# Four buffers for the transposed squares, four slots for the mirrored blocks, and side work moved in the first chunk and the last batch of an attention-and-experts kernel

## The chip, the core and the metric

The kernel runs on one core of a Trainium2 chip. The core has a matrix engine (TensorE, PE in the profile; PEld is its weight load), a vector engine (DVE), an activation engine (ACT), a general engine (POOL) and a sync engine (SP) that issues nearly all DMAs here, in one queue and in program order. The metric is the device time of one execution in microseconds. Before the change the median of three runs is 1546.55 us (1545.86 to 1554.03).

## What is computed

```python
# _attn_ref: batch 8, seq 2496, d_model 256, d_qk 64, all float32
scores = (1 / S) * np.matmul(z, z.transpose(0, 2, 1))
attn = np.maximum(scores, 0.0) ** 2
x = u * np.matmul(attn, v)                     # 19968 rows of 256
# _moe_ref: 8 experts, F = 1024, capacity 80
logits = x @ w_gate;  expert_idx = np.argmax(logits, axis=1)
# gate_w: the softmax probability of the chosen expert
for e in range(E):
    tok_idx = np.where(expert_idx == e)[0]     # cut to the 80 rows with ties broken as argpartition does
    h = np.maximum(x[tok_idx] @ w1[e], 0.0)
    out[tok_idx] = gate_w[tok_idx, None] * (h @ w2[e])
```

The matrix of scores is symmetric in z, and nothing but relu, square and a scale follows, so a block of squares below the diagonal is the transpose of one above it.

## The kernel before

The 2496 rows of a batch are padded to 20 tiles of 128. A **chunk** is four tiles (512 query columns), so a batch has five chunks; the names (b, qc) give batch and chunk, and there are 40. A chunk is worked off in ten **steps** r, each for a **pair** of key tiles (k = 2r, 2r+1). In the text "the second chunk" is qc = 1, and so on.

`scores(b, qc, k)` makes one pair. If the pair lies on or above the diagonal, PE multiplies (lines 300 and 301: two matmuls per tile, because z is split into a rounded part and a rest; `zc` holds the two in its halves, `zd` the same crossed), ACT does relu and square (304, 305), and the square `a` is split into `ah` (a rounding copy, on ACT or DVE) and `al` (a subtraction on DVE, line 310). Above the diagonal `mirror` also transposes the square on DVE (line 248) into a tile `x`, which four tiles of keys fill; the full `x` of 1 MB goes to DRAM as `y` (line 253), and is read back as a block `blk` (line 266) for the chunk in which it stands below the diagonal. There `mirrored` takes the place of the scores: ACT copies `blk` to `ah` (284), DVE subtracts to `al` (286). A block is named by (b, i, j): written in chunk j, used in chunk i. So chunk 0 writes (1,0), (2,0), (3,0), (4,0); chunk 1 writes (2,1), (3,1), (4,1); chunk 2 (3,2), (4,2); chunk 3 (4,3). `attend` multiplies `v` (split into two parts in `vt`) by `ah` and `al`: twelve matmuls for a pair and chunk (331 to 333).

Scores run two steps ahead (`LOOK = 2`). At each step the loop emits, in this order: the reads of blocks that are due, the scores of step i + 2, the attends of step i, the work on the chunk that just ended (`finished`: x = u * out, its rounding for the logits, a DMA transpose to 16-bit rows and their store, the logits, the gate), loads and splits for later chunks, the zeroing of a piece of the output, and in the last two chunks the early loads and splits of expert weights (`weights_ahead`, table `WAT`). The order on PE, ACT, DVE and SP is the order of this code (`manual_schedule`); each engine works off its own list and waits where a buffer or an input isn't ready.

The tiles that the change touches: `x` has two buffers (`sqpool`), a block takes one of six slots (`free`, `slot_of`), `y` has four buffers in DRAM, and a read of a block is emitted two steps after its write was. `prep_zd` fills `zd` of the next chunk with two DMAs from `zc` (lines 119, 120) at step 4. `prep_zc` (111) and `prep_v` (144, 145) split z and v. When the last chunk ends, `chunk_x_last`, `chunk_logits_last` and the last gate follow, and then the stage of the experts.

Of the kernel before, what the change touches and what calls it, by code (L numbers as in the profile page):

```python
# [8 lines left out]
F32 = mybir.dt.float32  # L9
# [10 lines left out]
P = 128  # L20
# [5 lines left out]
def attn_moe_kernel(ctx, tc, zT, uT, v, wg, w1, w2, out, seq, cap):  # L26
# [5 lines left out]
    nc = tc.nc  # L32
# [32 lines left out]
    NV, NW, NR = 6, 2, 5  # L65
    NA = 6
    SQ = 32
    weights = ExitStack()
    vpool = weights.enter_context(tc.tile_pool(name="vpool", bufs=NV))
    apool = weights.enter_context(tc.tile_pool(name="apool", bufs=1))  # L70
    sqpool = weights.enter_context(tc.tile_pool(name="sqpool", bufs=2))
    main = ExitStack()
# [100 lines left out]
    raw12 = upool.tile([P, 2, CH], F32, tag="ut", name="raw12")  # L173
    nc.sync.dma_start(out=raw12, in_=zT[0, :, CH:3 * CH].rearrange("p (j t) -> p j t", j=2))
    vraw0 = load_v(0, 0)


# [55 lines left out]


    a_t = {}

    half_t, blk, slot_of, free = {}, {}, {}, list(range(NA))
    n32 = P // SQ  # L240
    moving, now = [], [0]

    def mirror(b, i, j, t, a):

        if t == 0:
            half_t[b, i, j] = sqpool.tile([P, n32, QT, QT, SQ], F32, tag="x", name=f"x_{b}_{i}_{j}")
        x = half_t[b, i, j]
        V.transpose(out=x[:, :, :, t].rearrange("p n k s -> p k n s"), in_=a)  # L248
        if t < QT - 1:
            return  # L250

        y = dram.tile([n32, SQ, n32, QT * QT * SQ], F32, tag="y", name=f"y_{b}_{i}_{j}", bufs=4)
# [36 lines left out]
    def scores(b, qc, k):  # L289
# [262 lines left out]
    def wtile(name):  # L552
        if late.get("own"):
            pool, tag = late["own"], "w"
        else:
            i = n_early[0] % (NA + 2 + NV + NW)
# [39 lines left out]
    NP = NT // 2  # L596
    LOOK = 2
# [11 lines left out]
    def weights_ahead(b, qc, r):  # L609
        for p, raw in list(w_raw.items()):  # L610
            split_w(*p, w_raw.pop(p), V)
        if (b, qc, r) in WAT:
            if not places:

                assert len(free) == 3
                order = [free.pop() for _ in range(2)] + [slot_of[b, NQ - 1, j] for j in range(3)]
                places.extend([(apool, f"a{n}") for n in order[:2]] + [(sqpool, "x")] * 2)
                places.extend([(apool, f"a{n}") for n in order[2:4]] + [(vpool, "vt")] * 2)
                places.extend([(apool, f"a{n}") for n in order[4:] + free] + [(vpool, "vt")] * (NV - 2))
            p = WAT[b, qc, r]  # L620
            w_raw[p] = load_raw(*p)

    def finished(b, qc, r):

        if r == 0:
            chunk_hi(b, qc)
        elif r == 1:
            chunk_rest(b, qc)
            chunk_store(b, qc)
        elif r == 2:  # L630
            chunk_mid(b, qc)
        elif r == 3:
            chunk_lo(b, qc)
            chunk_store2(b, qc)
        elif r == 6:
            chunk_logits(b, qc)
            chunk_sum(b, qc)
# [6 lines left out]
        elif qc == 0 and b > 0:  # L644
            part = kb - BPB, kb
            if r == 2:
                count(*part)
            elif r == 4:
                up_to(*part)
                blocks(ps_m, "m", gp, oh, *part)  # L650
        elif b == B - 1 and qc == NQ - 2:
            part = kb, kb + BPB - 2
            if r == 7:
                gate_top(b, 0, NQ - 1)
                gate(b, 0, NQ - 1)
            elif r == 8:
                count(*part)
                up_to(*part)
                half()
            elif r == 9:  # L660
                blocks(ps_m, "m", gp, oh, *part)

    with tc.manual_schedule(engines={ET.PE, ET.Activation, ET.DVE, ET.SP}):
# [6 lines left out]
        z_raw[0, 2] = raw12[:, 1]  # L670
        z_raw[0, 3] = load_z(0, 3)
        v_raw[0, 1] = load_v(0, 1)
        constants()
        prev = None
        for i, (b, qc, r) in enumerate(steps):
            last = b == B - 1 and qc == NQ - 1
            now[0] = i
            mirror_back(i)
            if r == 0 and prev:
                chunk_x(*prev)  # L680
            if i + LOOK < len(steps):
                nb, nqc, nr = steps[i + LOOK]
                scores(nb, nqc, 2 * nr)
            if b == 0 and qc == 0:
                if r % 2 == 0 and r < 8:
                    g = r // 2 + 1
                    prep_v(0, g, v_raw.pop((0, g)), V, V)
                    if g + 1 < NQ:
                        v_raw[0, g + 1] = load_v(0, g + 1)
                if r % 2 == 1 and r < 6:  # L690
                    j = r // 2 + 2
                    prep_zc(0, j, z_raw.pop((0, j)))
                    if 3 < j + 1 < NQ:
                        z_raw[0, j + 1] = load_z(0, j + 1)
                if r == 8:
# [30 lines left out]
            if r == NP - 1:  # L726
                prev = b, qc
# [558 lines left out]
```

## Time and profile before

| | |
|---|---|
| median of three runs | 1546.55 us |
| the profiled execution | 1546.61 us |
| its span on the core | 1544.9 us |
| first chunk | 0 to 70.6 us |
| the other 38 chunks of the loop's steady part | 70.6 to 1401.7 us |
| last chunk | 1401.7 to 1444.8 us |
| end of the last chunk to the end of the span | 100.1 us |

The end of a chunk is the end of its last attend on PE (line 336). The profiled execution's time is 1.7 us more than its span, which is the work around it. All times in the rows below count from the span's start.

### The profile page before, as it was taken

How to read it: one execution, taken by the hardware profiler on the slowest of the kernel's cores; microseconds unless marked ns; L12 is line 12 of the kernel's file. 1: busy time of each engine (PE TensorE's matmuls, PEld its weight loads, DVE VectorE, ACT ScalarE, POOL GpSimd, SP SyncE). 2: the span in 40 equal slices, each digit the busy share in tenths (PEclk: the TensorE clock that was granted, in tenths of full speed). 3: DMA queues.
4: the chain of work that ended last, by engine and by line, in shares of the span. 5: the costliest groups of instructions: out<-in, count | busy, mean ns of one | idle time of the engine just before them, and what ended most of it. 6: DMA issues, size and time to landing. Idle time of an engine off the chain costs nothing. (4 is left out here: it accounts for less than half of the span.)

```text
span 1544.9 us, 19497 instructions
## 1 busy us (share of the span) xinstructions
PE 1416.7 (92%) x7083; PEld 1160.8 (75%) x7083; DVE 1085.0 (70%) x1538; ACT 979.9 (63%) x1254; POOL 48.5 (3%) x51
## 2 busy tenths in 40 slices
PE   6899999899989999899989999899989999898577
PEld 4688887788768877688768877788868887786356
DVE  5776777677866778567866767667767768666575
ACT  4476677557656677566666676566776667565254
POOL 1000000000000000000000000000000000000064
PEclk8899999999999999999999999999999999999699
DMA  4779859986898959887799959999599859988454
GB/s 143 211 212 246 197 146 186 250 226 161 247 196 233 234 135 193 234 241 189 199 190 249 218 135 219 230 237 225 155 210 245 226 132 232 218 218 254 83 182 142
DMA packets 300102, 311.97 MB, mean 202 GB/s; under 512 B 136184, under 2 KB 228224, under 8 KB 289760
## 3 DMA queue, kind: packets, MB, share of 16 engines
q1 hardware_dynamic: 299040, 309.11, 80.3%
q0 software_dynamic: 960, 1.56, 0.3%
q8 instruction: 57, 0.93, 0.3%
q14 instruction: 45, 0.37, 0.1%
HBM read 153.48 MB, written 126.46 MB: 181 GB/s over the span
## 5 line engine op out<-in xcount | busy, mean ns | idle before, releaser
L333 PE MATMUL acc<-al,vt 128*128 128x512 f32 (+1 forms) x1520 | 596.1, 392 | 48.0 <-DVE al L54 47.8
L331 PE MATMUL acc<-ah,vt 128*128 128x512 f32 (+1 forms) x1520 | 595.2, 392 | 1.4 <-ACT ah L284 0.8
L332 PE MATMUL acc<-ah,vt 128*128 128x512 f32 (+1 forms) x1520 | 593.1, 390 | 0.0
L54 DVE TENSOR_TENSOR al<-a,ah 128x1024 fp32r<-128x1024 f32 (+1 forms) x240 | 290.9, 1212 | 137.2 <-ACT ah L104 127.7
L333 PEld LDWEIGHTS acc<-al,vt 128*128 128x128 f32 x1520 | 291.1, 192 | 112.3 <-DVE al L54 58.8
L304 ACT ACTIVATE a<-s 128x512 f32<-128x512 f32 (+1 forms) x480 | 259.1, 590 | 147.3 <-PE s L301 135.6
L331 PEld LDWEIGHTS acc<-ah,vt 128*128 128x128 f32 x1520 | 291.7, 192 | 60.5 <-ACT ah L284 5.8
L332 PEld LDWEIGHTS acc<-ah,vt 128*128 128x128 f32 x1520 | 291.2, 192 | 54.9
L284 ACT CAST ah<-blk 128x1024 fp32r<-128x1024 f32 x160 | 166.1, 1047 | 180.9 <-DMA blk<-y 99.6
L248 DVE STREAM_TRANSPOSE x<-a 128x512 f32<-128x512 f32 x320 | 207.7, 687 | 76.2 <-DMA y<-x 76.2
L305 ACT ACTIVATE a<-a 128x1024 f32<-128x1024 f32 (+1 forms) x240 | 252.9, 1054 | 7.6
L54 DVE TENSOR_TENSOR al<-blk,ah 128x1024 fp32r<-128x1024 f32 x160 | 191.5, 1213 | 66.1 <-ACT ah L284 62.5
L301 PE MATMUL s<-zd,zc 128*128 128x512 f32 (+1 forms) x480 | 190.7, 397 | 16.3 <-DMA zd<-zc 16.3
L300 PE MATMUL s<-zc,zc 128*128 128x512 f32 x320 | 131.6, 411 | 21.0 <-DVE zc L54 19.5
L104 ACT CAST ah<-a 128x1024 fp32r<-128x1024 f32 x136 | 142.8, 1050 | 4.3
L106 DVE CAST ah<-a 128x1024 fp32r<-128x1024 f32 (+1 forms) x104 | 70.8, 681 | 92.1 <-ACT a L305 91.8
L301 PEld LDWEIGHTS s<-zd,zc 128*128 128x128 f32 x480 | 92.1, 192 | 35.3 <-DMA zd<-zc 19.0
L300 PEld LDWEIGHTS s<-zc,zc 128*128 128x128 f32 x320 | 60.8, 190 | 35.8 <-issue 21.1
L361 ACT CAST xb<-xf 128x1024 bf16<-128x1024 f32 (+1 forms) x39 | 40.0, 1027 | 58.6 <-DVE xf L350 58.6
L300 PE MATMUL s<-zc 128*128 128x512 f32 (+1 forms) x160 | 64.3, 402 | 1.7 <-ACT a L304 1.7
L145 DVE TENSOR_TENSOR vt<-vraw,vt 128x1024 fp32r<-128x1024 f32 (+1 forms) x39 | 45.6, 1168 | 25.6 <-ACT vt L104 25.2
L104 ACT CAST vt<-vraw 128x1024 fp32r<-128x1024 f32 (+3 forms) x50 | 40.4, 835 | 33.8 <-DMA vraw<-v 33.8
(158 smaller groups left out, 867.3 us busy)
## 6 DMA issues: line engine op xcount, KB each, us to landing
y<-x SPq DMA_DIRECT2D x80, 1024.0 KB, 7.4
blk<-y SPq DMA_DIRECT2D x320, 256.0 KB, 5.8
out<-idle SPq DMA_DIRECT2D x40, 512.0 KB, 6.6
vraw<-v SPq DMA_DIRECT2D x32, 512.0 KB, 6.2
ut<-uT SPq DMA_DIRECT2D x32, 512.0 KB, 4.6
xs<-xq SPq DMA_DIRECT2D x32, 512.0 KB, 6.5
wraw<-w SPq DMA_DIRECT2D x32, 512.0 KB, 5.5
zd<-zc SPq DMA_DIRECT2D x78, 128.0 KB, 7.1
```

Of the source, the lines that this page charges most:

```text
L54: V.tensor_tensor(out=o, in0=a, in1=b, op=op)
L104: eng.copy(out=o, in_=i)
L106: eng.tensor_copy(out=o, in_=i)
L248: V.transpose(out=x[:, :, :, t].rearrange("p n k s -> p k n s"), in_=a)
L284: nc.scalar.copy(out=natural(ah), in_=src)
L300: nc.tensor.matmul(s[:, :nq], zk, zc[:, :nq], start=True, stop=False)
L301: nc.tensor.matmul(s[:, :nq], zk, zd[:, :nq], start=False, stop=True)
L304: nc.scalar.activation(out=a[:, h, :nq], in_=s[:, :nq], func=AF.Relu)
L305: nc.scalar.activation(out=a[:, :, :nq], in_=a[:, :, :nq], func=AF.Square)
L331: nc.tensor.matmul(o, vt[:, t, 0, cs], ah, start=k == 0, stop=False)
L332: nc.tensor.matmul(o, vt[:, t, 1, cs], ah, start=False, stop=False)
L333: nc.tensor.matmul(o, vt[:, t, 0, cs], al, start=False, stop=False)
```

## The change

The buffers: `x` gets four instead of two, the slots of blocks become four instead of six, `y` in DRAM gets twelve. A read of a block is no longer emitted by age alone: reads go in the order of use, when the write is two steps old, when a slot is free, and at most twelve steps before the block is used; and `mirror_back` stands at the end of a step instead of its start. The list `to_read` runs, within a batch, in the order (1,0), (2,0), (2,1), (3,0), (3,1), and so on; its last number is the step in which the block's first pair is split.

```diff
-    NA = 6
+    NA = 4
+    NX = 4
-    sqpool = weights.enter_context(tc.tile_pool(name="sqpool", bufs=2))
+    sqpool = weights.enter_context(tc.tile_pool(name="sqpool", bufs=NX))
+    LOOK, AHEAD = 2, 12
+    to_read = [(b, i, j, ((b * NQ + i) * NT + j * QT) // 2 - LOOK)
+               for b in range(B) for i in range(NQ) for j in range(i)]
...
-        moving.append((b, i, j, y, now[0] + 2))
-
-    def mirror_back(i_step):
-
-        while moving and moving[0][4] <= i_step:
-            b, i, j, y, _ = moving.pop(0)
+        y_t[b, i, j] = y, now[0]
+
+    def mirror_back():
+
+        while to_read and free:
+            b, i, j, use = to_read[0]
+            if (b, i, j) not in y_t or y_t[b, i, j][1] + 2 > now[0] or use > now[0] + AHEAD:
+                return
+            to_read.pop(0)
+            y = y_t.pop((b, i, j))[0]
             slot_of[b, i, j] = free.pop(0)
...
-            if nb < B and r == 4:
+            if nb < B and r == 1:
                 prep_zd(nb, nqc)
...
+            mirror_back()
             if r == NP - 1:
```

In the first chunk z and v are loaded in other pieces and earlier, `zc` is made two steps before the scores that use it and ahead of them on DVE, the rounding copy of `v` goes from DVE to ACT, the first subtraction of `v` from POOL to DVE, and the three `ah` that DVE made in the first chunk of each batch (`ON_V`) go to ACT in batch 0.

```diff
-        on_v = k // QT == qc or (qc, k) in ON_V
+        on_v = k // QT == qc or (qc, k) in ON_V and b > 0
...
         prep_zd(0, 0, raw0)
+        prep_zc(0, 1, raw12[:, 0])
         scores(0, 0, 0)
+        prep_v(0, 0, vraw0, nc.scalar, V)
         scores(0, 0, 2)
-        prep_v(0, 0, vraw0, nc.scalar, nc.gpsimd)
-        prep_zc(0, 1, raw12[:, 0])
...
+            if (b, qc) == (0, 0) and r in (0, 2, 4):
+                prep_zc(0, r // 2 + 2, z_raw.pop((0, r // 2 + 2)))
             if i + LOOK < len(steps):
...
-                    prep_v(0, g, v_raw.pop((0, g)), V, V)
+                    prep_v(0, g, v_raw.pop((0, g)), nc.scalar, V)
...
-                if r == (7 if b == 0 and qc == 0 else 1):
+                if r == 1:
```

In the last batch the early weights come at other steps (ten pieces: four in the fourth chunk and six in the fifth, where two and eight were), the tiles that they take over are listed anew (`places`), and the work on the fourth chunk, its logits and its gate come one to two steps earlier.

```diff
-    at_w = [(NQ - 2, 6), (NQ - 2, 8)] + [(NQ - 1, r) for r in range(8)]
+    at_w = [(NQ - 2, r) for r in (2, 4, 6, 8)] + [(NQ - 1, r) for r in range(1, 7)]
...
+        at_end = b == B - 1 and qc == NQ - 2
...
-            if r == 7:
+            if r == 5:
                 gate_top(b, 0, NQ - 1)
+            elif r == 6:
                 gate(b, 0, NQ - 1)
```

What this does to the lists of the engines, at three places. The first is SP in the second chunk of batch 1 and the end of its first chunk; `y_2_1` is the write of block (2,1), `blk_2_1` its read, `gall` the gate's values, `xq` the transposed 16-bit rows, `out` the zeroing. Before:

```order
L266 DMA blk_3_0_1968<-y_3_0_1898 32x4x512 x4
L253 DMA y_4_0_1989<-x_4_0_1927 128x2048
L489 DMA xs<-gall 128x20x1 x2
L266 DMA blk_4_0_2043<-y_4_0_1989 32x4x512 x4
L400 DMA_TRANSPOSE xq_0_2126<-xf_0_2065 128x8x128 x2
L99 DMA zraw_2129<-zT 128x512
L158 DMA ut_1_2165<-uT 128x2x512
L253 DMA y_2_1_2183<-x_2_1_2145 128x2048
L409 DMA xs<-xq_0_2126 128x8x256
L543 DMA wtab<-wb_2242 80x256
```

Now, in the same stretch and a little further:

```order
L261 DMA y_4_0_1983<-x_4_0_1921 128x2048
L501 DMA xs<-gall 128x20x1 x2
L412 DMA_TRANSPOSE xq_0_2115<-xf_0_2054 128x8x128 x2
L100 DMA zraw_2118<-zT 128x512
L120 DMA zd_2_2120<-zc_2_1146 64x512
L121 DMA zd_2_2120<-zc_2_1146 64x512
L159 DMA ut_1_2157<-uT 128x2x512
L261 DMA y_2_1_2175<-x_2_1_2137 128x2048
L421 DMA xs<-xq_0_2115 128x8x256
L555 DMA wtab<-wb_2234 80x256
L261 DMA y_3_1_2253<-x_3_1_2205 128x2048
L278 DMA blk_2_1_2268<-y_2_1_2175 32x4x512 x4
```

The reads of (3,0) and (4,0) no longer stand ahead of the write of (2,1), the two DMAs of `zd` do, and the read of (2,1) now stands behind the write of (3,1) (before, it stood ahead of it).

The second is DVE in the first chunk of batch 0, from the first pair's `ah` on. Before:

```order
L106 CAST ah_0_0_149<-a_0_0_139 128x1024
L54 TENSOR_TENSOR al_0_0_151<-a_0_0_139,ah_0_0_149 128x1024
L106 CAST ah_0_2_163<-a_0_2_153 128x1024
L54 TENSOR_TENSOR al_0_2_165<-a_0_2_153,ah_0_2_163 128x1024
L111 CAST zc_1_170<-raw_109 128x512
L54 TENSOR_TENSOR zc_1_170<-raw_109,zc_1_170 64x512
```

Now:

```order
L112 CAST zc_1_144<-raw_109 128x512
L54 TENSOR_TENSOR zc_1_144<-raw_109,zc_1_144 64x512
L107 CAST ah_0_0_157<-a_0_0_147 128x1024
L54 TENSOR_TENSOR al_0_0_159<-a_0_0_147,ah_0_0_157 128x1024
L146 TENSOR_TENSOR vt_0_161<-vraw_0_111,vt_0_161 128x4x256
L107 CAST ah_0_2_174<-a_0_2_164 128x1024
```

`zc_1`, which the third pair's scores need, went from behind two pairs to ahead of the first, and the subtraction of `v` came in from POOL.

The third is SP in the fifth chunk of batch 0, where `zd` of the next batch's first chunk is made. Before:

```order
L99 DMA zraw_1470<-zT 128x512
L131 DMA vraw_2_1475<-v 128x4x256
L158 DMA ut_4_1494<-uT 128x2x448
L409 DMA xs<-xq_3_1467 128x8x256
L131 DMA vraw_3_1517<-v 128x4x256
L119 DMA zd_0_1535<-zc_0_536 64x512
L120 DMA zd_0_1535<-zc_0_536 64x512
```

Now:

```order
L100 DMA zraw_1469<-zT 128x512
L132 DMA vraw_2_1474<-v 128x4x256
L120 DMA zd_0_1476<-zc_0_525 64x512
L121 DMA zd_0_1476<-zc_0_525 64x512
L159 DMA ut_4_1496<-uT 128x2x448
L421 DMA xs<-xq_3_1466 128x8x256
L132 DMA vraw_3_1519<-v 128x4x256
```

`zd` moved ahead of three transfers.

## Rows read from the trace of the kernel before

**Rows 1.** Waits, whole span: us in total, times, longest us.

```profile
DVE x L248 <- DMA y<-x: 76.2, 14, 9.3
PE acc L333 <- DVE al L54: 47.8, 22, 6.4
PE s L300 <- DVE zc L54: 19.5, 4, 8.2
PE s L301 <- DMA zd<-zc: 16.3, 7, 2.9
```

**Rows 2.** Windows, second chunks of batches 1 to 7: us, busy (count), PEclk, DMA.

```profile
410.60:455.90 45.30, 38.05 (x181) 29.77 (x180) 31.61 (x55) 29.13 (x39) 0.00 (x0) 0.93 0.91 205
...
sum 309.20, PE 265.91 PEld 208.09 DVE 220.16 ACT 203.76 POOL 0.00; mean PE 37.99 PEld 29.73 DVE 31.45 ACT 29.11 POOL 0.00
```

**Rows 3.** Windows, second chunk of batch 0.

```profile
70.60:105.40 34.80, 34.80 (x175) 28.70 (x175) 26.93 (x36) 27.29 (x35) 0.00 (x0) 1.00 0.81 212
```

**Rows 4.** Timeline of DVE, second chunk of batch 2: start, us, what [idle before].

```profile
430.05 1.30 DVE L248 STREAM_TRANSPOSE x<-a 128x512 f32<-128x512 f32 x2
...
437.79 1.30 DVE L248 STREAM_TRANSPOSE x<-a 128x512 f32<-128x512 f32 x2
...
449.52 1.30 DVE L248 STREAM_TRANSPOSE x<-a 128x512 f32<-128x512 f32 x2 [9.32 <-DMA y<-x]
```

**Rows 5.** Timeline of SP's DMA queue, the same chunk.

```profile
419.53 7.96 SPq L489 DMA_DIRECT2D xs<-gall  x2
...
431.15 9.57 SPq L400 DMA_TRANSPOSE xq<-xf  x2
...
441.94 0.39 SPq L253 DMA_DIRECT2D y<-x  x1
...
449.51 1.76 SPq L266 DMA_DIRECT2D blk<-y  x4
```

**Rows 6.** Timeline of ACT, start of the third chunk of batch 2.

```profile
459.04 1.05 ACT L284 CAST ah<-blk 128x1024 fp32r<-128x1024 f32 x1 [12.86 <-DMA blk<-y]
```

**Rows 7.** Windows, fifth chunks of batches 0 to 6.

```profile
345.60:375.60 30.00, 28.39 (x159) 25.60 (x159) 21.91 (x24) 20.20 (x25) 0.00 (x0) 1.00 0.90 221
...
sum 223.50, PE 206.81 PEld 185.26 DVE 152.98 ACT 141.15 POOL 0.00; mean PE 29.54 PEld 26.47 DVE 21.85 ACT 20.16 POOL 0.00
```

**Rows 8.** Windows, first chunk of batch 0 from its first attend on.

```profile
17.80:70.60 52.80, 41.48 (x148) 32.70 (x147) 34.78 (x54) 24.16 (x30) 0.00 (x0) 0.82 0.66 183
```

**Rows 9.** Timeline of all engines, first chunk: first relu, first attend.

```profile
6.39 1.09 ACT L304 ACTIVATE a<-s 128x512 f32<-128x512 f32 x2 [2.19 <-PE s L301]
...
17.81 0.63 PE L331 MATMUL acc<-ah,vt 128*128 128x512 f32 x1
```

**Rows 10.** Lines by form: count, busy us, mean ns, idle before.

```profile
L54 DVE TENSOR_TENSOR al<-a,ah 128x1024 fp32r<-128x1024 f32 x224 | 273.4, 1221 | 136.1 <-ACT ah L104 127.7
...
L305 ACT ACTIVATE a<-a 128x1024 f32<-128x1024 f32 x224 | 237.6, 1061 | 7.1
L248 DVE STREAM_TRANSPOSE x<-a 128x512 f32<-128x512 f32 x320 | 207.7, 687 | 76.2 <-DMA y<-x 76.2
...
L104 ACT CAST ah<-a 128x1024 fp32r<-128x1024 f32 x136 | 142.8, 1050 | 4.3
...
L54 DVE TENSOR_TENSOR zc<-zraw,zc 64x512 fp32r<-64x512 f32 x38 | 26.2, 689 | 1.3
...
L111 DVE CAST zc<-zraw 128x512 fp32r<-128x512 f32 x38 | 15.9, 417 | 5.0 <-DMA zraw<-zT 5.0
```

**Rows 11.** Windows, third chunk of batch 2.

```profile
455.90:489.30 33.40, 33.40 (x168) 27.50 (x167) 22.82 (x27) 23.14 (x29) 0.00 (x0) 0.99 0.90 254
```

**Rows 12.** Windows, last chunk.

```profile
1401.70:1444.80 43.10, 31.55 (x156) 25.17 (x156) 31.16 (x48) 21.62 (x26) 0.00 (x0) 0.92 0.69 179
```

**Rows 13.** Timeline of ACT around the end of the last chunk.

```profile
1451.92 1.04 ACT L584 CAST w1h<-wraw 128x1024 fp32r<-128x1024 f32 x1 [12.60 <-DMA wraw<-w]
```

**Rows 14.** Timeline of DVE, the last chunk's x.

```profile
1454.14 1.27 DVE L350 SCALAR_TENSOR_TENSOR xf<-acc,ut 128x256 f32<-128x256 f32 x4
```

More of the change, by code (lines that the diff above doesn't have):

```diff
@@ L173, in attn_moe_kernel @@
     raw12 = upool.tile([P, 2, CH], F32, tag="ut", name="raw12")
-    nc.sync.dma_start(out=raw12, in_=zT[0, :, CH:3 * CH].rearrange("p (j t) -> p j t", j=2))
+    nc.sync.dma_start(out=raw12[:, 0], in_=zT[0, :, CH:2 * CH])
     vraw0 = load_v(0, 0)
+    nc.sync.dma_start(out=raw12[:, 1], in_=zT[0, :, 2 * CH:3 * CH])
+    vraw1 = load_v(0, 1)
+    raw34 = xpool.tile([P, 2, CH], F32, tag="xf", name="raw34")
+    nc.sync.dma_start(out=raw34, in_=zT[0, :, 3 * CH:].rearrange("p (j t) -> p j t", j=2))
     ident = const.tile([P, P], F32, name="ident")
@@ L232, in zero_out @@
                           in_=zero.rearrange("p (o d) -> p o d", o=1).broadcast_to([P, r1 - r0, D]))
+    LOOK, AHEAD = 2, 12
     a_t = {}
-    half_t, blk, slot_of, free = {}, {}, {}, list(range(NA))
+    half_t, y_t, blk, slot_of, free = {}, {}, {}, {}, list(range(NA))
     n32 = P // SQ
-    moving, now = [], [0]
+    now = [0]
+    to_read = [(b, i, j, ((b * NQ + i) * NT + j * QT) // 2 - LOOK)
+               for b in range(B) for i in range(NQ) for j in range(i)]
     def mirror(b, i, j, t, a):
@@ L250, in mirror @@
             return
-        y = dram.tile([n32, SQ, n32, QT * QT * SQ], F32, tag="y", name=f"y_{b}_{i}_{j}", bufs=4)
+        y = dram.tile([n32, SQ, n32, QT * QT * SQ], F32, tag="y", name=f"y_{b}_{i}_{j}", bufs=12)
         nc.sync.dma_start(out=y.rearrange("g p h f -> (g p) (h f)"),
                           in_=x.rearrange("p h k t s -> p (h k t s)"))
-        moving.append((b, i, j, y, now[0] + 2))
-    def mirror_back(i_step):
-        while moving and moving[0][4] <= i_step:
-            b, i, j, y, _ = moving.pop(0)
+        y_t[b, i, j] = y, now[0]
[6 more added lines that the diff above has]
+            y = y_t.pop((b, i, j))[0]
             slot_of[b, i, j] = free.pop(0)
@@ L555, in wtile @@
         else:
-            i = n_early[0] % (NA + 2 + NV + NW)
+            i = n_early[0] % (NA + NX + NV + NW)
             n_early[0] += 1
@@ L596, in attn_moe_kernel @@
     NP = NT // 2
-    LOOK = 2
     ON_V = {(0, 8), (0, 12), (0, 16)}
     order_w = [(0, 1), (0, 2), (1, 1), (1, 2), (2, 1)]
-    at_w = [(NQ - 2, 6), (NQ - 2, 8)] + [(NQ - 1, r) for r in range(8)]
+    at_w = [(NQ - 2, r) for r in (2, 4, 6, 8)] + [(NQ - 1, r) for r in range(1, 7)]
     WAT = {(B - 1,) + at: (*order_w[n // 2], n % 2) for n, at in enumerate(at_w)}
@@ L613, in weights_ahead @@
             if not places:
[L615 to L619, printed above, removed]
+                xt, vv = (sqpool, "x"), (vpool, "vt")
+                nb = B * NQ * (NQ - 1) // 2
+                a4 = [(apool, f"a{n % NA}") for n in range(nb - NA, nb)]
+                places.extend([xt, xt, xt, vv, a4[0], vv, xt, a4[1], a4[2], vv, a4[3], vv, vv, vv])
             p = WAT[b, qc, r]
@@ L629, in finished @@
             chunk_store(b, qc)
-        elif r == 2:
+        elif r == 3:
+            chunk_store2(b, qc)
+        if r == 1 and at_end or r == 2 and not at_end:
             chunk_mid(b, qc)
-        elif r == 3:
+        if r == (2 if at_end else 3):
             chunk_lo(b, qc)
-            chunk_store2(b, qc)
-        elif r == 6:
+        if r == (4 if at_end else 6):
             chunk_logits(b, qc)
@@ L650, in finished @@
                 blocks(ps_m, "m", gp, oh, *part)
-        elif b == B - 1 and qc == NQ - 2:
+        elif at_end:
             part = kb, kb + BPB - 2
-            if r == 7:
+            if r == 5:
                 gate_top(b, 0, NQ - 1)
+            elif r == 6:
                 gate(b, 0, NQ - 1)
@@ L665, in attn_moe_kernel @@
         prep_zd(0, 0, raw0)
+        prep_zc(0, 1, raw12[:, 0])
         scores(0, 0, 0)
+        prep_v(0, 0, vraw0, nc.scalar, V)
         scores(0, 0, 2)
-        prep_v(0, 0, vraw0, nc.scalar, nc.gpsimd)
-        prep_zc(0, 1, raw12[:, 0])
-        z_raw[0, 2] = raw12[:, 1]
-        z_raw[0, 3] = load_z(0, 3)
-        v_raw[0, 1] = load_v(0, 1)
+        v_raw[0, 1] = vraw1
+        z_raw.update({(0, 2): raw12[:, 1], (0, 3): raw34[:, 0], (0, 4): raw34[:, 1]})
         constants()
@@ L677, in attn_moe_kernel @@
             now[0] = i
-            mirror_back(i)
             if r == 0 and prev:
                 chunk_x(*prev)
+            if (b, qc) == (0, 0) and r in (0, 2, 4):
+                prep_zc(0, r // 2 + 2, z_raw.pop((0, r // 2 + 2)))
             if i + LOOK < len(steps):
@@ L686, in attn_moe_kernel @@
                     g = r // 2 + 1
-                    prep_v(0, g, v_raw.pop((0, g)), V, V)
+                    prep_v(0, g, v_raw.pop((0, g)), nc.scalar, V)
                     if g + 1 < NQ:
                         v_raw[0, g + 1] = load_v(0, g + 1)
[L690 to L694, printed above, removed]
                 if r == 8:
```

## The prediction

> **What bounds the kernel now.** I read the windows chunk by chunk first, because the shares of the whole span average stages with different limits. The second chunk of batch 0 is the yardstick [rows 3]: 34.80 us, PE busy all of them, full granted clock, no wait. So PE is the bound wherever nothing else is late, and the question for every other chunk is how far it lies above such a time. The same chunk of batches 1 to 7 takes 309.20 us in all, 44.2 each [rows 2]. Two things are lost there: PE stands idle (45.3 long, 38.05 busy), and part of the rest runs at the lower of its two clock levels (granted mean 0.93, so more busy time for nearly the same instructions). The fifth chunks show the same at a smaller scale [rows 7]: the best has 28.39 us of work, the seven take 223.5. Then the ends: the first chunk of batch 0 has 41.48 us of work in 52.8 at a clock of 0.82 [rows 8], the last chunk 31.55 in 43.1 [rows 12].
>
> Next the waits [rows 1]. Three of them fit these places: DVE's transposes wait 76.2 us for the write of `y` (the buffer of `x` isn't free), and PE's wait for `al` (47.8) hangs on that; scores wait for `zd` (16.3) and `zc` (19.5). The timeline of one second chunk shows the first in full [rows 4, 5]. Block (2,1) is transposed by 431.3, but its write is issued only at 441.94: SP, in order, sat in the gate's store (7.96 us), a read behind it, and the DMA transposes (9.57). The write lands at 449.5, the transposes of (4,1), which need the same buffer, start there after 9.32 us, everything behind them on DVE is late, and PE with it. ACT then waits for the read of (2,1), issued at 449.51, until 459.04 [rows 6].
>
> **The change part by part.** The sum is made against the profiled execution, 1546.6 us (1544.9 of span and 1.7 around it), which is the median of the runs shown to 0.1 us.
>
> *Four buffers for x.* A transposed block reuses the buffer of the fourth before it, written a chunk ago, so the 76.2 us of DVE's wait have no cause left. What PE needs of a second chunk is 34.80 plus the count of the batch before, six small matmuls (181 against 175), say 35.0. Seven chunks: 309.2 - 245.0 = **64.2 us** saved if nothing else is late. Below that, DVE: it is busy 31.6 us in these chunks, of 35, so it fits, with 3 us to spare; if it lost 1 to 1.5 us a chunk by its waits for ACT the term would be 55. Above, 68: third chunks begin at full clock too.
>
> *Blocks read later, in order of use.* In the list of SP two reads of 1 MB leave the stretch ahead of the write of (2,1), and the transposes, which were held while they ran, come earlier. The write can then go at about 432, as soon as its `x` is there, and land at 440 (it took 7.6 us [rows 5]). But its read now stands behind the write of (3,1), whose `x` was done at 439.1 [rows 4], and behind the zeroing: issue at 440 to 441, with 1.5 MB ahead in the queue. At the 205 and 254 GB/s of rows 2 and 11 these take 7.3 to 5.9 us and the read itself 4.9 to 3.9: it lands at 450 to 453. It is needed so: third chunk at 410.6 + 35.0 = 445.6; two steps of twelve matmuls without scores, 2 x 2.7 (34.80 us over 175 matmuls, 24 of them the small ones of the logits, so between 0.20 and 0.23 each; I take 0.225 [rows 3]); the scores of the next pair, 0.9; less ACT's copy of 1.05 and DVE's 1.22 [rows 10], of which PE's first matmuls hide 0.5: about 450.1. So between nothing and 2 us of wait in each of seven batches, 0 to 14 in all. I take half, **7 us lost**, and no loss of clock, as the fifth chunk with 1.61 us of idleness (30.00 less 28.39) kept 1.00 [rows 7]. The blocks (1,0), (3,2) and (4,3) are read five steps ahead of their use, as (2,1) is, but only (3,2) has a write put ahead of its read, and the fourth chunks are the least loaded of the later ones; nothing is put down for it, and up to 1 us in each of eight chunks if its cover of about a step is gone. All others are read eleven steps ahead or more.
>
> The Trainium skill (DMA: Bandwidth & Descriptors, section "Queues, rings and completion order") says that each DMA engine takes the descriptors of a ring in their order. By that rule the read cannot overtake the 1.5 MB, the upper end holds in every batch, and the sum would be 7 us longer, 1443, which lies within the forecast's own range. The rows shown hold no read with a write directly ahead that would confirm it.
>
> *`zd` at step 1.* Its two DMAs of 128 KB leave SP's place behind three transfers. The waits go if it lands 3 us sooner; the largest was 2.9 [rows 1], and the three transfers are 1.4 MB, some 6 us at the 221 GB/s of rows 7. What each fifth chunk can give is its distance from 28.4: 223.5 - 198.8 = 24.7. I take **23**, bounds 12 (half of them still late) and 25. It costs nothing where it goes: the buffer of `zd` was last read in the chunk before.
>
> *First chunk.* The first relu starts at 6.39 [rows 9]; with 1.09 for two of them, 1.06 for the square, some 0.7 for `ah` on DVE (an estimate between a transpose of half the size, 0.69, and ACT's copy, 1.05) and 1.22 for `al` the first pair is split at 10.5; the subtraction of `v`, now DVE's (1.22), ends by 11.7, and the third pair's scores no longer wait for `zc_1`. So the first attend moves from 17.81 to about 12. Then the step's pace. ACT: 1.09 + 1.06 + 1.05 and half a copy of `v`, 3.7. DVE: 1.22 + 1.37 for two transposes, and every second step 1.22 for `v` and 1.11 for `zc` (0.42 + 0.69), 3.75 [rows 10]. PE: sixteen matmuls, 3.6. All three are nearly level, so eight steps at 3.75, two of 2.7, and 2.4 for a first step at the lower clock: 12 + 30 + 5.4 + 2.4 = 50. Before 70.6: **20.6 saved**. PE's wait for `zc` of 19.5 goes, since it is made two steps ahead. Bounds: 46 at PE's own pace; 56 if each of the three loads of `v` that now stand behind a 1 MB write comes 2 us late, and ACT, which now does the copies of `v`, passes that on.
>
> *Last batch.* Two pieces of weights leave the last chunk, and the gate comes two steps earlier, so the count no longer waits at its end. The price now is the last piece: ACT waits 12.60 us for it until 1451.92 [rows 13], DVE makes the last `x` only at 1454.14 [rows 14], 9.3 after PE ended, and all that follows hangs on it. Piece and gate move one to two steps of 4.3 us forward: 4.3 to 8.6, and DVE's `x` with them unless PE's own end is later. If the last piece no longer matters, 9.3, and PE's 11.55 of idleness on top: 20. I take **10**, bounds 4 and 20.
>
> Sum: 64.2 + 23 + 20.6 + 10 - 7 = 110.8; 1546.6 - 110.8 = **1436 us**. With each term at its bound on the same side, two thirds of the way, this case reaches from 1415 to 1458.
>
> **The rivals.** *All hidden.* No block late, PE's pace in the first chunk, the last piece early: 1436 - 7 - 4 - 10 - 3 = 1412. For it speaks that third chunks carry 254 GB/s with PE never idle [rows 11]; against it that three engines are level in the first chunk. *The wait moves to the block's read.* If SP's list still lets (2,1) go at 441.94, it lands at 459.0 [rows 6] against a need at 450.1: 8.9 idle, and 3.2 of clock (38.05 - 34.8) come back, 12 a batch. 7 x 12 = 84 in place of 7: 1513. For it: the gate's store and the transposes keep their place ahead of that write. Against: two reads ahead of them are gone. *The side work gives half.* `zd`, first chunk and last batch are held by DMA traffic rather than by their place: half of 53.6 is lost, 1463. *Slower.* The same traffic must go through in less time: the DMA share is 0.90 to 0.91 already [rows 2, 11]. With four slots and use order each block of (2,1), (3,2) and (4,3) stands behind later writes; if the queue can't keep up, each read comes late and PE's clock falls each time. 24 such reads have to cost 4.9 us each to eat 118 us of gain (110.8 + 7); from 5 us on it is slower. At 6 us it is 1429 + 144 = 1573. Against it: that third chunk, with two reads inside it, shows no idle PE at this share.
>
> The skill's same page (section "Specifications") puts HBM at about 358 GB/s for a core. By that figure 254 is 71% and the queue has room, so "slower" would fall away and the lost 7 us too: 1429. The row's share of 0.90 says otherwise, and I go by the row.
>
> **How the numbers follow.** Forecast 0.55, all hidden 0.17, half 0.10, wait moved 0.13, slower 0.05. The time is the first's, 1436. The range 1408 to 1478 holds the forecast, all hidden and half, and leaves out the moved wait and slower. No change, within 0.5% (7.7 us, about what can be told here), would need losses to cancel 111 us almost exactly: 0.01. So faster by more 0.94, slower by more 0.05.
>
> **What would show it.** Right: no wait of DVE's transposes for `y`; second chunks of 35 to 36 us at a clock of 1.00; fifth chunks of 28.4 to 29; first attend near 12 and first chunk's end near 50; the last `x` within a few us of PE's end. The new wait, if there is one, is ACT at the third chunk's (2,1). Wrong: second and third chunks together still over 74, PE's waits for `al` of a mirrored block in third or fourth chunks, or a first chunk over 56.

## The result, and the profile after

The changed kernel takes 1480.17 us (median of 4 runs, 1479.06 to 1484.24); the kernel before, run beside it, 1546.83. The ratio is 0.9564, with a 95% interval of 0.953 to 0.9598. The forecast was 1436 in a range of 1408 to 1478: the direction was right, the gain is 67 us where 111 were forecast, and the time lies 2 us outside the range. Below, a chunk lasts from the end of one chunk's last accumulating matmul to that of the next, and all differences are between the two profiled executions (spans 1544.9 and 1478.4).

First the waits over the whole span, the view of [rows 1] for the changed kernel:

```profile
engine line waited for: us in total, times, longest us
ACT ah L296 <- DMA blk<-y: 65.9, 21, 5.7
ACT vt L105 <- DMA vraw<-v: 65.3, 23, 4.4
PE s L312 <- ACT a L316: 35.9, 26, 15.9
ACT w1h L596 <- DMA wraw<-w: 35.2, 7, 18.3
```

DVE's wait for the write of `y` (76.2 before) is gone from the list, and so is PE's for `zd`. What grew are PE's wait for `a` of ACT (3.2 before), once 15.9 us long, and ACT's waits for loads of `v` (33.8 before) and of weights (26.0 before). Then the windows: the second chunks of batches 1 to 7 [rows 2], two of them and the sum (columns: start:end in us, length, then busy us of PE, PEld, DVE, ACT, POOL with instruction counts, PE's granted clock, DMA share, GB/s):

```profile
550.80:587.50 36.70, 35.93 (x180) 28.55 (x179) 30.76 (x52) 28.87 (x38) 0.00 (x0) 1.00 0.90 223
1221.60:1256.80 35.20, 35.20 (x180) 28.78 (x180) 29.27 (x50) 27.94 (x37) 0.00 (x0) 1.00 0.95 218
sum 255.30, PE 251.00 PEld 200.42 DVE 213.51 ACT 200.86 POOL 0.00; mean PE 35.86 PEld 28.63 DVE 30.50 ACT 28.69 POOL 0.00
```

The clock is 1.00 in all seven, and they take 255.3 us, 53.9 less than before. The fifth chunks of batches 0 to 6 [rows 7], the one of batch 2 and the sum:

```profile
483.60:515.00 31.40, 29.15 (x159) 25.36 (x159) 20.94 (x23) 18.68 (x24) 0.00 (x0) 1.00 0.99 248
sum 218.80, PE 204.62 PEld 179.31 DVE 147.82 ACT 132.25 POOL 0.00; mean PE 29.23 PEld 25.62 DVE 21.12 ACT 18.89 POOL 0.00
```

Only 4.7 us are gained, at a DMA share of 0.99 where the best before had 0.90. Last, the fourth chunk of the last batch, before:

```profile
1370.40:1401.70 31.30, 31.30 (x159) 25.29 (x157) 17.35 (x20) 18.01 (x22) 0.00 (x0) 1.00 0.84 227
```

And now, with the last chunk [rows 12] below it:

```profile
1289.80:1339.50 49.70, 33.77 (x159) 27.30 (x158) 21.69 (x24) 21.26 (x25) 0.00 (x0) 0.83 0.78 185
1339.50:1389.40 49.90, 33.64 (x158) 28.60 (x157) 28.25 (x47) 19.22 (x24) 0.00 (x0) 0.79 0.63 145
```

PE never stood in the first of these before; the second took 43.1. What follows the last chunk fell from 100.1 to 89.0.

So the 66.5 us of span are: second chunks 53.9, first chunk 20.6 (it ends at 50.0), fifth chunks 4.7, third chunks of batches 1 to 7 3.4 (234.1 to 230.7), less 14.1 lost in the last batch (18.4 and 6.8 lost, 11.1 won behind) and 2.0 in the first chunks of batches 1 to 7 (247.5 to 249.5). Fourth chunks of the other batches and the rest of batch 0 did not move.

The loss in the last batch can be read in three timelines. SP, ahead of the fourth chunk and in it (columns: start us, us held, queue, line, transfer, count):

```profile
1287.80 10.13 SPq L278 DMA_DIRECT2D blk<-y  x12
1298.87 8.01 SPq L412 DMA_TRANSPOSE xq<-xf  x2
1306.97 0.54 SPq L120 DMA_DIRECT2D zd<-zc  x1
1307.56 0.59 SPq L121 DMA_DIRECT2D zd<-zc  x1
1308.24 1.98 SPq L278 DMA_DIRECT2D blk<-y  x4
1310.27 0.43 SPq L159 DMA_DIRECT2D ut<-uT  x1
1310.74 0.47 SPq L586 DMA_DIRECT2D wraw<-w  x1
```

ACT in the same stretch (in brackets the idle time before and what ended it):

```profile
1299.69 1.04 ACT L296 CAST ah<-blk 128x1024 fp32r<-128x1024 f32 x1
1319.06 1.04 ACT L596 CAST w1h<-wraw 128x1024 fp32r<-128x1024 f32 x1 [18.33 <-DMA wraw<-w]
1320.01 1.08 ACT L316 ACTIVATE a<-s 128x512 f32<-128x512 f32 x2
```

And PE:

```profile
1304.33 0.39 PE L313 MATMUL s<-zd,zc 128*128 128x512 f32 x1
1320.65 0.80 PE L312 MATMUL s<-zc 128*128 128x512 f32 x1 [15.93 <-ACT a L316]
```

Three block reads go out in one burst and hold SP for 10 us, the transposes for 8 more. The first piece of weights, which the program gives out at step 2, is issued at 1310.74, when PE has used up all that was prepared (1304.7). ACT had come to the split of that piece at 1300.7, and the relu that PE needs stands behind it in ACT's order. In the last chunk the same thing happens once more: ACT waits 10.85 us, until 1383.02, for a piece issued at 1374.43 behind the gate's store, and the count's copy behind it holds PE for 9.24 us. ACT's row, then PE's:

```profile
1383.02 1.04 ACT L596 CAST w1h<-wraw 128x1024 fp32r<-128x1024 f32 x1 [10.85 <-DMA wraw<-w]
```

```profile
1384.23 0.27 PE L550 MATMUL wp<-upper,oh 128*64 128x128 bf16 x1 [9.24 <-ACT tot L513]
```

### The profile page after: what moved, and what is told of

It is laid out like the page before. It is cut to its first block, busy times and chain, and to the rows that moved or that the text cites. A ratio compares the mean times of both kernels' runs of the same rounds, so it can differ in the third digit from the quotient of the medians.

```text
span 1478.4 us, 19494 instructions
## 1 busy us (share of the span) xinstructions
PE 1396.2 (94%) x7083; PEld 1144.3 (77%) x7083; DVE 1078.6 (73%) x1530; ACT 983.7 (67%) x1263; POOL 45.6 (3%) x50
## 5 line engine op out<-in xcount | busy, mean ns | idle before, releaser
L345 PEld LDWEIGHTS acc<-al,vt 128*128 128x128 f32 x1520 | 287.8, 189 | 67.9 <-DVE al L54 15.3
L343 PEld LDWEIGHTS acc<-ah,vt 128*128 128x128 f32 x1520 | 288.4, 190 | 60.8 <-ACT ah L296 4.6
L344 PEld LDWEIGHTS acc<-ah,vt 128*128 128x128 f32 x1520 | 288.4, 190 | 55.5 <-DVE vt L146 2.0
L54 DVE TENSOR_TENSOR al<-blk,ah 128x1024 fp32r<-128x1024 f32 x160 | 192.3, 1214 | 81.7 <-ACT ah L296 80.0
L313 PE MATMUL s<-zd,zc 128*128 128x512 f32 (+1 forms) x480 | 187.4, 391 | 0.1
L105 ACT CAST ah<-a 128x1024 fp32r<-128x1024 f32 x139 | 146.0, 1050 | 4.4
L105 ACT CAST vt<-vraw 128x1024 fp32r<-128x1024 f32 (+3 forms) x56 | 45.0, 831 | 65.3 <-DMA vraw<-v 65.3
```

What stands on the lines that cost most here:

```text
L54: V.tensor_tensor(out=o, in0=a, in1=b, op=op)
L105: eng.copy(out=o, in_=i)
L313: nc.tensor.matmul(s[:, :nq], zk, zd[:, :nq], start=False, stop=True)
L343: nc.tensor.matmul(o, vt[:, t, 0, cs], ah, start=k == 0, stop=False)
L344: nc.tensor.matmul(o, vt[:, t, 1, cs], ah, start=False, stop=False)
L345: nc.tensor.matmul(o, vt[:, t, 0, cs], al, start=False, stop=False)
```

## The experiments

Each changes the changed kernel, except where another kernel is named; times are single runs beside the kernel before, except the last. How far single runs can be trusted: the changed kernel's four runs span 5 us, and one kernel that was profiled twice (the last two below) has its seven fifth chunks at 209.5 and at 206.0.

**Weights back at their former steps.**

```diff
-    at_w = [(NQ - 2, r) for r in (2, 4, 6, 8)] + [(NQ - 1, r) for r in range(1, 7)]
+    at_w = [(NQ - 2, 6), (NQ - 2, 8)] + [(NQ - 1, r) for r in range(8)]
```

> The changed kernel with the ten early weight pieces back at their former steps (6 and 8 of the last batch's fourth chunk, 0 to 7 of its last chunk); everything else of the change stays, the earlier logits and gate among it. Theory (the pieces taken at steps 2 and 4 stand on SP behind the block reads and the transposes, and ScalarE, in order, waits for them): the last batch's fourth chunk falls from 49.8 us to 31.3 to 32, the 15.9 us wait of TensorE in it is gone; the last chunk, 49.9 us now, lies at 43 to 47, what follows it at 89 to 100; the whole about 1462 us (1452 to 1470). Rival A (the earlier logits and gate hold ScalarE, not the weights): the fourth chunk stays above 45 us and the whole above 1475. Rival B (the wait only moves on to the next piece that is late): the fourth chunk falls, the last chunk rises by as much, the whole stays at 1475 to 1485.

1463.32 us. The fourth chunk of the last batch:

```profile
1288.00:1319.10 31.10, 31.09 (x158) 25.30 (x156) 16.96 (x19) 16.56 (x20) 0.00 (x0) 1.00 1.07 227
```

It is back at 31.1 us, so the early pieces are what held ACT, and the earlier logits and gate, which are still there, are not (rival A falls). Nor did the wait merely move on: the last chunk is 3.5 us longer than as changed, the fourth 18.6 shorter (rival B falls). The last chunk was mis-forecast: 53.4 us, not 43 to 47, with 89.2 behind it. Last two chunks and what follows make 173.7, against 188.6 as changed and 174.5 before: the weights cost 15 us, and moving the rest of the last batch's side work gains 0.8.

**The split two steps behind the load.**

```diff
-        for p, raw in list(w_raw.items()):
-            split_w(*p, w_raw.pop(p), V)
+        for p, (raw, i) in list(w_raw.items()):
+            if now[0] >= i + 2:
+                split_w(*p, w_raw.pop(p)[0], V)
...
-            w_raw[p] = load_raw(*p)
+            w_raw[p] = load_raw(*p), now[0]
```

> The changed kernel with each early weight piece loaded where the change loads it, but split into its two halves two steps later instead of one. Theory (SP itself comes to the load some 11 us late, so one more step, 3.1 us of TensorE, buys only that much for each step): the 15.9 us wait of the last batch's fourth chunk shrinks by about one step, to 9 to 13 us, and the chunk to 43 to 47 us; the whole 1470 to 1476. Rival (a plain landing time of 5 to 8 us, which two steps would cover): the fourth chunk at 31.3 to 33 us and the whole at 1462 or below.

1468.46 us; PE's wait 11.59, the chunk 45.8: one step's worth, as the theory has it, so SP's lateness is more than one step. The whole is below the 1470 to 1476 forecast, since the last chunk fell by 17.0 us to 32.9, which was not expected (PE's wait at the count is 1.45 in place of 9.24); what follows it grew by 8.5 to 97.5, so half of that stays won.

**`zd` back at step 4.** (`if nb < B and r == 1:` is `r == 4:` again.)

> The changed kernel with the two copies of zd back at step 4 of a chunk, all else as changed. Theory (in the fifth chunks TensorE now waits for ScalarE, which waits for the v pieces, and the copies of zd are no longer what comes last; moved back they are issued behind the v loads and become late again): the seven fifth chunks of batches 0 to 6, 218.7 us now, rise to 222 to 230, with waits of 1 to 3 us for DMA zd in them; the whole 1483 to 1492. Rival A (the earlier zd is itself what delays v in the queue): the fifth chunks fall below 216. Rival B (zd's step doesn't matter any more): 217 to 221, the whole 1478 to 1482.

1485.64 us. The sums of the fifth, first and second chunks:

```profile
sum 233.80, PE 208.86 PEld 184.57 DVE 153.89 ACT 140.42 POOL 0.00; mean PE 29.84 PEld 26.37 DVE 21.98 ACT 20.06 POOL 0.00
sum 243.50, PE 243.50 PEld 200.56 DVE 212.65 ACT 184.97 POOL 0.00; mean PE 34.79 PEld 28.65 DVE 30.38 ACT 26.42 POOL 0.00
sum 250.70, PE 249.30 PEld 201.24 DVE 212.69 ACT 196.37 POOL 0.00; mean PE 35.61 PEld 28.75 DVE 30.38 ACT 28.05 POOL 0.00
```

The fifth chunks lie above the 222 to 230 expected, so the step does win 15.0 us there. But the first and second chunks of the next batches are shorter without it, 243.5 and 250.7 against 249.5 and 255.3: 10.6 of the 15.0 are handed back. The whole is 5 us longer, about what the changed kernel's own runs span.

**Blocks read at most eight pairs ahead.** (`LOOK, AHEAD = 2, 12` becomes `2, 8`.)

> The changed kernel with blocks read at most 8 pairs ahead instead of 12, so that the reads of the last chunk's blocks are spread over the fourth chunk and don't go out three at once. Theory (the three reads at the end of the third chunk fill the queue, and what they push back is late in the fourth and fifth chunks): the 10.2 us that SP is held by 12 reads in one go falls to 3 to 5 us; in the last batch's fourth chunk the first weight piece is issued 5 to 10 us earlier and the wait of 15.9 us falls to 6 to 11; fifth chunks of batches 0 to 6 216 to 220 (218.7 now), since the bytes in them are no fewer; the whole 1469 to 1476. Rival A (the reads' order matters for nothing but themselves): 1478 to 1482 with the 15.9 us wait as it is. Rival B (later reads are late for their own use): new waits of ScalarE for blocks of 3 us and more in the fifth chunks, fifth chunks over 225, the whole over 1485.

1465.15 us. SP now sends the reads in two parts ahead of the last batch's fourth chunk, and the first weight piece goes out 16 us after the first of them, where it was 23:

```profile
1280.26 5.08 SPq L278 DMA_DIRECT2D blk<-y  x8
1286.39 7.94 SPq L412 DMA_TRANSPOSE xq<-xf  x2
...
1296.28 0.48 SPq L586 DMA_DIRECT2D wraw<-w  x1
```

PE's wait in that chunk is 6.54, as expected. The fifth chunks were not: I held the bytes to be the limit there and expected 216 to 220. The view of the fifth chunks, that of batch 2, the last and the sum of all seven:

```profile
481.00:511.00 30.00, 28.75 (x160) 25.51 (x159) 20.93 (x23) 18.78 (x24) 0.00 (x0) 1.00 0.98 239
1148.90:1178.20 29.30, 28.52 (x160) 25.53 (x159) 20.98 (x23) 18.73 (x24) 0.00 (x0) 1.00 0.99 251
sum 206.50, PE 199.63 PEld 178.55 DVE 146.61 ACT 131.32 POOL 0.00; mean PE 28.52 PEld 25.51 DVE 20.94 ACT 18.76 POOL 0.00
```

12 us come back at much the same share and rate. Loads of `v` land 7.4 us after issue where they took 8.9 (medians of the whole span). But the premise that the bytes are no fewer failed: length times rate, summed over the seven rows of each view, gives 51.1 MB where the changed kernel has 53.6, and at its 245 GB/s these 2.4 MB are 10 us. The fourth chunks before them carry as much more (50.6 MB against 48.2) in the same 218 us, at a share of 1.05 to 1.09 in both kernels. So the other order moved bytes into the fourth chunks, where they cost nothing; whether the bytes or what stands ahead of the loads of `v` sets the fifth chunks, the run does not tell.

**Both.**

> The changed kernel with blocks read at most 8 pairs ahead and each early weight piece split two steps after its load. Theory (two causes that add up: SP reaches the weight pieces late because three block reads go out at once, and ScalarE is given too little slack behind the load): the last batch's fourth chunk at 32 to 37 us (49.8 as changed, 40.9 with the reads alone, 45.8 with the split alone), the last chunk at 33 to 40, fifth chunks of batches 0 to 6 at 204 to 209; the whole 1444 to 1453. Rival (both act on the same 10 us, so the better of them is all there is): fourth chunk 40 us or more, the whole 1455 to 1462.

1452.21 us; fourth chunk 37.8 (a little over), last 34.4, fifth chunks 207.8. The two causes add up: the whole is 28.0 us below the changed kernel, and the edits alone are 15.0 and 11.7 below it.

**Both, and the weights at their former steps.**

> As the one before, and the ten weight pieces back at their former steps (6 and 8 of the fourth chunk, 0 to 7 of the last). Theory (taking the pieces earlier buys nothing while ScalarE has two steps of slack): the fourth chunk 31.1 to 31.5 us, the last chunk 33 to 40, the whole 1441 to 1450. Rival (the earlier pieces do buy time at the end: the last chunk or what follows it is longer by 5 to 10 us, as 53.4 against 49.9 us in the last chunk when the pieces were put back alone): the whole 1451 to 1460.

1456.95 us, in the rival's range. Fourth chunk 31.1, last chunk 40.5, 99.2 behind it. The two last chunks and what follows take 170.8, and 170.0 with the early pieces; the rest of the difference lies in the fifth and third chunks (2.8 and 2.3 us), where the kernels don't differ. So the rival's 5 to 10 us are there at the end (7.5), but the fourth chunk gives 6.6 of them back: when the pieces are taken makes next to nothing, once ACT needn't wait for them.

**Transposes behind the loads of step 1.** (To the two edits of "both", `chunk_store` is moved from `finished` to the end of step 1, ahead of `mirror_back`.)

> Blocks at most 8 ahead, split two steps after the load, and the two transposes of a finished chunk issued behind the loads of step 1 (z, v, zd, weight piece) instead of ahead of them. Theory (SP is held 6 to 10 us by the two transposes, and all that step 1 loads stands behind them): ScalarE's wait for v, 51.6 us with the reads at most 8 ahead, falls below 25; fifth chunks of batches 0 to 6 from 206.7 to 199 to 204; the last batch's fourth chunk below 33; the whole 1435 to 1446. Rival (the queue's bytes are what delays v, not SP): fifth chunks 205 to 209, no more than 3 us off the kernel without this step.

1465.94 us, 14 more than without it; fifth chunks 224.1, ACT's wait for `v` 57.3 in place of 54.9. Neither the theory nor the rival foresaw it. The order of issue in the fifth chunk of batch 2:

```profile
488.72 0.38 SPq L100 DMA_DIRECT2D zraw<-zT  x1
491.04 0.39 SPq L132 DMA_DIRECT2D vraw<-v  x1
...
492.67 6.37 SPq L412 DMA_TRANSPOSE xq<-xf  x2
...
501.47 1.49 SPq L132 DMA_DIRECT2D vraw<-v  x2
```

The first load of `v` does go earlier, but 2 us pass ahead of it in which SP issues nothing, and the transposes take their 6.4 us all the same and now stand ahead of the next loads of `v`, which ACT needs a few steps later. The profile puts the pause down to DVE's split of an earlier piece of `v` (1.9 us), so to the buffer that the load fills; no run took it away.

**The kernel before, with `zd` at step 1 alone.** (`if nb < B and r == 4:` becomes `r == 1:`.)

> The kernel before with one edit of the change alone: the two copies of zd issued at step 1 of a chunk instead of step 4. Theory (the 23 us forecast for this step are there in the former traffic, where the last chunk's blocks are read later, and were lost to the block reads in the changed kernel): fifth chunks of batches 0 to 6 from 223.5 to 200 to 206, no wait for DMA zd, the whole 1524 to 1531 against 1543 to 1547. Rival (with zd early, the fifth chunk is bounded by ScalarE waiting for v in any traffic): fifth chunks 214 to 220, the whole 1538 to 1543.

1545.56 us against 1544.73: nothing is gained, which neither the theory nor the rival had. And yet the fifth chunks do what the forecast said:

```profile
346.00:374.10 28.10, 28.10 (x159) 25.66 (x158) 21.54 (x23) 19.58 (x24) 0.00 (x0) 1.00 0.97 236
sum 200.10, PE 198.53 PEld 179.16 DVE 147.26 ACT 133.35 POOL 0.00; mean PE 28.36 PEld 25.59 DVE 21.04 ACT 19.05 POOL 0.00
```

200.1 where the forecast has 200.5. Its waits over the whole span say where the 23 us went:

```profile
ACT ah L284 <- DMA blk<-y: 116.9, 17, 14.1
DVE x L248 <- DMA y<-x: 92.1, 14, 11.1
```

DVE's wait for `y` grows from 76.2 to 92.1 [rows 1], the second chunks from 309.2 to 317.0, the first chunks from 247.5 to 261.5. PE came earlier to a transfer that came no earlier.

**`v` made ready on GpSimd.**

```diff
-                        prep_v(b + 1, g, v_raw.pop((b + 1, g)), nc.scalar, V)
+                        prep_v(b + 1, g, v_raw.pop((b + 1, g)), nc.gpsimd, nc.gpsimd)
```

> Blocks at most 8 ahead, split two steps after the load, and the v pieces of the next batch made ready on GpSimd (both the copy and the subtraction) instead of ScalarE and VectorE. Theory (what the earlier zd gained in the fifth chunk is handed back in the next batch's first two chunks because ScalarE, in order, stands still for the v pieces and begins the batch behind; with that wait on an engine that nobody stands behind it stays won): ScalarE's wait for v (54.9 us) falls to near the first batch's alone (under 12), fifth chunks of batches 0 to 6 from 207.9 to 198 to 203, first chunks of batches 1 to 7 from 249.8 to 243 to 246, second chunks from 255.5 to 248 to 253; the whole, 1452 without this step, 1430 to 1442. Rival (GpSimd takes 3.2 us for a subtraction of this size, so a piece is ready later and the first chunk waits for it, or VectorE runs slower beside it): first chunks at 250 or more with waits for v, the whole above 1448.

1463.58 us, 11 more than without it: the rival, by its second half. First chunks 254.2. ACT waits for `v` only in the first batch (3.4 us of the 54.9 are left), and yet the first chunks grew. That does not bear the theory out, but it does not clear ACT's backlog either, since another engine was slowed at the same time. This is seen on GpSimd and then on DVE, both in the fifth chunk of batch 2:

```profile
509.42 2.74 POOL L146 TENSOR_TENSOR vt<-vraw,vt 128x1024 fp32r<-128x1024 f32 x1
```

```profile
510.00 3.24 DVE L54 TENSOR_TENSOR al<-a,ah 128x1024 fp32r<-128x1024 f32 x1
```

DVE's subtraction, 1.22 us while GpSimd is idle, takes 3.24 while GpSimd's runs. (The Trainium skill, SBUF — State Buffer, section "Who interferes with whom", has a VectorE instruction with two SBUF inputs contend with a GpSimd instruction that reads SBUF, and calls the port pair that the two share an exclusive lock; the two rows agree, as DVE's ends 1.1 us after GpSimd's, about its own length.)

**`zd` at step 3.** (To "both", `r == 1` becomes `r == 3`.)

> Blocks at most 8 ahead, split two steps after the load, and zd copied at step 3 (step 1 as changed, step 4 before). Theory (a wait for zd in the fifth chunk is mostly a rest in which ScalarE and VectorE catch up, so where in the chunk it stands moves time between chunks and little of the whole): fifth chunks of batches 0 to 6 rise from 207.9 to 212 to 222, first and second chunks of batches 1 to 7 fall by 5 to 11 together (505.3 now); the whole 1450 to 1459. Rival (every us of the fifth chunk stays won): the whole rises as the fifth chunks do, to 1460 or more.

1471.26 us: the rival. Fifth chunks 232.3 (24.4 more), first chunks 243.4 (6.4 less), second 256.3. Here three quarters of what the early `zd` wins stays won, where the kernel with twelve pairs ahead kept a third.

**Six pairs ahead**, with the split two steps behind.

> Split two steps after the load and blocks read at most 6 pairs ahead (8 in the kernel compared with, 12 as changed). Theory (12 to 8 took the three reads apart, which is all there is to take): fifth chunks of batches 0 to 6 205 to 209 (207.9 at 8), the last batch's fourth chunk 36 to 39, third chunks of batches 0 to 7 up by 0 to 6 us in all since the first blocks of a chunk come later; the whole 1450 to 1458. Rival (the later the reads the better for v and the weights): fifth chunks at 203 or below, the fourth chunk below 35, the whole below 1447.

1448.69 us, between the two: the fourth chunk 32.9, fifth chunks 209.5 (at 8: 207.8; the same kernel below: 206.0), third chunks 230.6, the end of the kernel 169.2 from the fourth chunk of the last batch on.

**The same, timed.**

> The kernel with blocks at most 6 pairs ahead and the split two steps after the load once more, now timed in three rounds against the kernel before. Theory (the single time of 1448.7 us was no accident: the last batch is some 19 us shorter than in the changed kernel, the fifth chunks some 9 us): 1446 to 1452 us, 0.936 to 0.941 of the kernel before. Rival (the order of landings in the fifth chunks varies from run to run): runs that lie 5 us and more apart, a median up to 1458.

1447.33 us (median of 4 runs, 1446.68 to 1448.56) against 1543.82; ratio 0.9383, interval 0.9357 to 0.9409. It is faster than both the kernel before and the changed one. Its longest waits:

```profile
ACT ah L296 <- DMA blk<-y: 61.7, 23, 5.1
ACT vt L105 <- DMA vraw<-v: 51.4, 22, 4.2
ACT w1h L596 <- DMA wraw<-w: 22.2, 10, 9.4
PE s L312 <- ACT a L316: 14.0, 21, 2.5
```

PE's longest wait for `a` is 2.5 us, where it was 15.9.

## Why the prediction was wrong, step by step

| step | forecast, us | measured, us |
|---|---|---|
| four buffers for x (second chunks) | -64.2 | -53.9 |
| read of block (2,1) (third chunks) | +7 | -3.4 |
| `zd` at step 1 (fifth chunks) | -23 | -4.7 |
| first chunk | -20.6 | -20.6 |
| last batch | -10 | +14.1 |
| first chunks of batches 1 to 7 | 0 | +2.0 |

- **Last batch: the step that failed.** I priced only what leaves the last chunk (bounds 4 and 20 won) and not where the pieces go: behind twelve block reads and two transposes on SP, with ACT in order behind them. The prediction costed SP's list for `zd` and for (2,1), but put "two pieces of weights leave" at nothing for the chunk that receives them. The weights back gave 16.9 us of the whole, 15 of them here. The part that was right is the last `x`, which now follows PE's end directly: DVE waits for PE's `acc` until 1388.42, not for weights, and 11.1 us are won behind the last chunk. But 6.8 of these stand in the last chunk again, where a late piece now stops PE by way of the count, so 4.3 are won in the place that was priced, the lower bound. With every term at its worst bound the sum comes to 1475: it took a term that turned its sign to reach 1480. (Two thirds of the way to the bounds is 1418 to 1462, not the 1415 to 1458 that the prediction gives.)
- **`zd` at step 1: right in its place, wrong in the sum.** The kernel before with this edit alone puts the fifth chunks at 200.1. In the changed kernel 12 of the 18 us that are missing go with the reads that the change lets go twelve pairs ahead (they come back with eight), of which I counted only what they clear ahead of (2,1). And an idle stretch taken from PE need not shorten the kernel: alone, the same edit gave back 22 of its 23 us in the next two chunks, where DVE waits for `y`; I added up terms from separate chunks as if none fed the next.
- **Four buffers for x: mechanism right, 10 us too much.** No wait of DVE for `y`, clock 1.00. Five of the ten may be handed over from the fifth chunk (250.7 with `zd` at step 4 in the changed kernel; at step 3 with eight pairs ahead they did not fall). What PE waits for in these chunks is DVE and ACT, as the lower bound of 55 had it: the one at 550.8 has 0.5 us of wait for `al` and 0.2 for `a`. In all seven PE is idle 4.3 us (255.3 less 251.0 busy); the other 6 are in its busy time, 35.86 in the mean where I took 35.0.
- **The read of (2,1) costs nothing.** The third chunks are 33 us and PE has no wait in them; the 3.4 us gained are near the 3.8 that the upper bound of the first term had for third chunks at full clock. In batch 2 the read is issued from 411.78 on, 28.1 us into the second chunk (29.4 to 30.4 forecast) and only 0.9 us behind the write of (3,1). Its block is there at 423.67, 11.9 us later, within the 10 to 12 forecast. ACT's row there: `[5.68 <-DMA blk<-y]`, a wait that PE does not feel: the read came earlier and the third chunk began later (35.7 against 35.0) than forecast, so the block lands 4.3 us into it, just ahead of the 4.5 at which it was needed. By the Trainium skill's rule that a ring is served in order (DMA: Bandwidth & Descriptors, section "Queues, rings and completion order") the prediction had the upper end of its wait in every batch. The 11.9 us do not speak against that rule; what was wrong is what hung on it, the time of issue and of need.
- **First chunk: right in its mechanism, exact by luck.** It ends at 50.0 against 50, but the first attend came at 10.34 against 12, and from there it took 39.7 us where 37.8 had been added up, 1.64 of them one wait of PE for `v`. The two errors cancel.
- **Rivals.** "The side work gives half" named DMA traffic, which two of its three terms met, and the nearest time (1463), but not that a term would turn its sign. The slower case had the price of late reads (4.9 us each) where in fact ACT's longest wait for a block is 5.7 and, outside the last batch, PE stands under 1 us behind any of them.

Left open: why fifth chunks stay at 206 to 210 us with eight or six pairs ahead, when they reach 200.1 in the former traffic. Fewer bytes pass there (46.5 MB, against 51.1 with eight and 49.4 in the timed kernel with six), but from eight to six pairs bytes left these chunks and no time was won. Taking the transposes behind the loads of step 1 made these chunks longer (224.1). Open is also which order of engines makes first chunks pay 6 us for an early `zd`; the one theory tried for it, ACT's backlog from `v`, was not borne out, in a run that slowed DVE as well.

## What to carry to other kernels

When a load is moved earlier, price the queue at its new place and everything that stands in order behind the instruction that consumes it: here a piece of weights, needed only after the last chunk, stopped the matmuls for 16, and one more step between load and use, with fewer reads let out at once, won 33 us. A wait removed is worth only what the next rendezvous lets through, so terms of one loop are not to be summed before asking what each passes on. And a DMA share near 1 does not say that no more bytes can pass: fourth chunks at 1.05 to 1.09 carried 48, 51 and 52 MB (twelve, eight and six pairs ahead) in the same 218 us.

## What the runs showed of the hardware that was not expected

One short pause cost more than its idle time shows. In the changed kernel, PE at the start of a first chunk:

```profile
355.07 0.39 PE L312 MATMUL s<-zc,zc 128*128 128x512 f32 x1
355.30 0.39 PE L313 MATMUL s<-zd,zc 128*128 128x512 f32 x1
356.02 0.50 PE L312 MATMUL s<-zc,zc 128*128 128x512 f32 x1 [0.33 <-ACT a L316]
356.35 0.40 PE L313 MATMUL s<-zd,zc 128*128 128x512 f32 x1
356.59 0.39 PE L343 MATMUL acc<-ah,vt 128*128 128x512 f32 x1
```

Starts are 0.23 us apart; across the pause 0.72, and 0.33 for the next. The wait is given as 0.33 and takes 0.59 (0.49 and 0.10) at a granted clock of 1.00. The longer pause of 15.93 us left the chunk at a granted mean of 0.83, so more of it at the lower of the two levels: its PE work is 33.8 us, against 31.1 without the pause. And GpSimd beside DVE, in the experiment above, raised DVE's 160 subtractions of mirrored blocks from 1214 to 1341 ns in the mean.
